# Scoring a quarter of the keys on VectorE instead of TensorE in a one-token attention decode

## Chip, cores, metric

One core of a Trainium2 chip. The metric is the device time of one execution, in microseconds; where several runs are given, the median. In the profile PE is TensorE (PEld its weight loads), DVE is VectorE, ACT is ScalarE, POOL is GpSimd, SP is SyncE, which here issues the loads. The granted clock is the share of its full speed at which the profile says that TensorE was allowed to run. A packet is one piece of a transfer; those of K and V have 16 KB each.

## The reference

```python
q = (x @ wq).reshape(1, 1, 32, 128).transpose(0, 2, 1, 3)      # x: 1 x 512
scores = einsum("bhqd,bhkd->bhqk", q, k_cache) * 128 ** -0.5   # k_cache: 1 x 32 x 65536 x 128, bf16
p = softmax(scores)
a = einsum("bhqk,bhkd->bhqd", p, v_cache).reshape(1, 1, 4096) @ wo
b = (silu(x @ w_gate) * (x @ w_up)) @ w_down                   # 512 -> 1792 -> 512
out = g * a + (1 - g) * b                                      # g = sigmoid(sum(x * gate_w))
```

K and V are 537 MB each. Everything else is small. One token reads all of it once, so the floor is the time of the loads.

## The kernel before

Per head there are 512 key blocks of 128 keys, in eight chunks of 64 blocks; a chunk of K or V is one 2 MB load into a slot of a ring. K lies with the keys on the partitions, and this kernel transposes it for the scores: TensorE transposes eight blocks into a PSUM bank, VectorE or ScalarE (in turn) copies the bank to SBUF, and TensorE multiplies each transposed block by q. For the values, V is the stationary operand as it lies. A "step" of the PE program is one group of eight transposes, eight value matmuls of an earlier head and eight score matmuls of the group two steps back.

```python
NSLOT = 9; NPT = 5; NKT = 6; LAG_QK = 2; LAG_PV = 12
...
jobs = [wq, wq, k0, wg, wu, wd, k1, ..., k8, v0, k9, v1, ...]      # (shortened) V eight chunks behind K
for i, job in enumerate(jobs):                                     # SP
    if i >= NSLOT:
        w(*free_of(jobs[i - NSLOT]))      # k: all transposed;  v: all value matmuls of the chunk done
    sp.dma_start(view(job), source(job)).then_inc(ld[i % NSLOT], 16)
...
for g in range(1, NG, 2):                                          # ScalarE: odd groups
    h, r = divmod(g, GPH)
    if r == 9 and h >= 1:
        softmax(h - 1)                    # waits for nbias (GpSimd), then Exp over 512 columns
    w("tdone", g + 1)
    ...
    nc.scalar.activation(KT[:, g % NKT, :], kt_ps(g), ACT.Copy, bias=0.0).then_inc(sm["ev_a"], 1)   # L244
...
for g in range(0, NG, 2):                                          # VectorE: even groups
    if r == 4 and h >= 1:
        top(h - 1)                        # reduce_max of the head's scores, then GpSimd's all-reduce
    ...
    nc.vector.tensor_copy(KT[:, g % NKT, :], kt_ps(g)).then_inc(sm["ev_d"], 1)                      # L307
...
for g in range(n_steps):                                           # TensorE
    if g < NG: transposes(g)              # L352
    if 0 <= g - first_pv < NG: values(g - first_pv)                # L383, first_pv = GPH + LAG_PV
    if 0 <= g - LAG_QK < NG: scores(g - LAG_QK)                    # L366
    if g == mid: ...                      # out_proj of heads 0..30, after the first group of the last V chunk
```

Of the kernel before, what the change touches and what calls it, by code (L numbers as in the profile page):

```python
# [4 lines left out]

P = 128
GB = 8
NSLOT = 9
NPT = 5
NKT = 6  # L10
LAG_QK = 2
LAG_PV = 12

ALU = mybir.AluOpType
ACT = mybir.ActivationFunctionType
BF16 = mybir.dt.bfloat16
F32 = mybir.dt.float32
AX_X = mybir.AxisListType.X
# [4 lines left out]
def bass_gated_mix__mha_block_cached__swiglu_ffn__decode_kernel(  # L23
# [13 lines left out]
    _, H, S, Dh = A_k_cache.shape  # L37
# [3 lines left out]
    Dc = D // 128  # L41
    FC = F // 128
    NC_H = S // P
    assert NC_H <= 512
    CB = min(64, NC_H)
    NCH = NC_H // CB
    GPC = CB // GB
    GPH = NC_H // GB
    NG = H * GPH
    SCALE = float(Dh) ** -0.5  # L50
    SLOT = CB * 128

    with ExitStack() as ctx:
        def sb(name, shape, dt):
            return ctx.enter_context(nc.sbuf_tensor(name, shape, dt))
# [28 lines left out]
        oTn = sb("oTn", [P, max(H, 16)], BF16)  # L84
        fin = sb("finrow", [P, D], BF16)
        pcol = sb("pcol", [P, 2, NC_H], BF16)
        KT = sb("KT", [P, NKT, GB * 128], BF16)
        ring = sb("ring", [P, NSLOT, SLOT], BF16)

# [18 lines left out]
        for s in range(NK):  # L108
            jobs.append(("k", s))
            if s == 0:  # L110
                jobs += [("wg", 0), ("wu", 0), ("wd", 0)]
            if s >= NCH:
                jobs.append(("v", s - NCH))
        for s in range(NK - NCH, NK):
            if s == NK - NCH + min(2, NCH - 1):
                jobs += [("wo", i) for i in range(NOW)]
            jobs.append(("v", s))
# [16 lines left out]
        def source(job):  # L134
# [7 lines left out]
            if kind == "v":  # L142
# [3 lines left out]
        ld = [sem(f"ld{i}") for i in range(NSLOT)]  # L146
        names = ("s_x s_id0 s_ident s_ones s_xT s_xTb s_z s_e1 s_c s_q s_qTb s_h s_sig s_gu s_b s_brow "
                 "tdone ev_d ev_a qkdone pvdone s_mx s_ar s_nb expdone s_L s_li s_otn s_otl s_a s_a1 "
                 "s_fin s_out s_bs").split()
        sm = {n: sem(n) for n in names}  # L150

        def free_of(job):
            kind, i = job
            if kind == "wq":
                return "s_q", 1
            if kind in ("wg", "wu"):
                return "s_h", 1
            if kind == "wd":
                return "s_b", 1
            if kind == "k":  # L160
                return "tdone", (i + 1) * GPC
            if kind == "v":
                return "pvdone", i + 1
            raise AssertionError(kind)

        class Waits:
# [13 lines left out]

        def ev_of(g):

            return ("ev_d" if g % 2 == 0 else "ev_a"), g // 2 + 1

        def kt_ps(g):
            return psT[:, g % NPT, :].bitcast(BF16)
# [3 lines left out]
        @block.sync  # L190
        def _(sp):
            w = Waits(sp)
            sp.dma_start(xrow[0:1, :], A_x.rearrange("a b d -> (a b) d")).then_inc(sm["s_x"], 16)
            sp.dma_start(gwrow[0:1, :], gate_w.rearrange("(a d) -> a d", a=1)).then_inc(sm["s_x"], 16)
            for i, job in enumerate(jobs):
                if i >= NSLOT:
                    w(*free_of(jobs[i - NSLOT]))
                sp.dma_start(view(job), source(job)).then_inc(ld[i % NSLOT], 16)  # L198
            w("s_fin", 1)
            sp.dma_start(out.rearrange("a b d -> (a b) d"), fin[0:1, :]).then_inc(sm["s_out"], 16)  # L200
            w("s_out", 16)
# [17 lines left out]
        @block.scalar  # L219
        def _(act):  # L220
            w = Waits(act)
            w("s_z", 1)
            nc.scalar.activation(sc[0:1, 1:2], sc[0:1, 0:1], ACT.Exp, scale=-1.0).then_inc(sm["s_e1"], 1)

            def softmax(h):
                w("s_nb", h + 1)
                if h >= 2:
                    w("pvdone", (h - 1) * NCH)
                nc.scalar.activation(pcol[:, h % 2, :], psS[:, h % 2, 0:NC_H], ACT.Exp,  # L229
                                     bias=nbias[:, h:h + 1], scale=SCALE,  # L230
                                     accum_out=rsum[:, h:h + 1]).then_inc(sm["expdone"], 1)

            for g in range(1, NG, 2):
                if g == 2 * GPC + 1 or (2 * GPC + 1 >= NG and g == NG - 1):
                    w("s_h", 1)
                    nc.scalar.activation(hbuf[:, 0, 0:FC], psS[:, 1, 0:FC], ACT.Exp,
                                         scale=-1.0).then_inc(sm["s_sig"], 1)
                h, r = divmod(g, GPH)
                if r == 9 and h >= 1:
                    softmax(h - 1)  # L240
                w("tdone", g + 1)
                if g >= NKT:
                    w("qkdone", g - NKT + 1)
                nc.scalar.activation(KT[:, g % NKT, :], kt_ps(g), ACT.Copy, bias=0.0).then_inc(sm["ev_a"], 1)  # L244
            softmax(H - 1)

        @block.vector
        def _(dve):
# [14 lines left out]
                                           accum_out=sc[0:1, 0:1]).then_inc(sm["s_z"], 1)  # L263
            w("s_xT", 1)
            nc.vector.tensor_copy(xTb[:, 0:Dc], psS[:, 0, 0:Dc]).then_inc(sm["s_xTb"], 1)
            w("s_e1", 1)
            chain(nc.vector.tensor_scalar_add(sc[0:1, 2:3], sc[0:1, 1:2], 1.0))
            settle()
# [6 lines left out]
            def ffn():  # L275
# [7 lines left out]
                nc.vector.tensor_tensor(guT[:, 0:FC], hbuf[:, 0, 0:FC], psS[:, 1, 16:16 + FC],  # L283
                                        ALU.mult).then_inc(sm["s_gu"], 1)

            def top(h):
                w("qkdone", (h + 1) * GPH)
                nc.vector.reduce_max(mxs[:, h:h + 1], psS[:, h % 2, 0:NC_H], AX_X).then_inc(sm["s_mx"], 1)  # L288

            def ffn_out():  # L290
# [2 lines left out]
                nc.vector.tensor_scalar(brow[0:1, :], psO[0:1, 0:D], sc[0:1, 4:5], None,  # L293
                                        ALU.mult).then_inc(sm["s_brow"], 1)

            for g in range(0, NG, 2):
                if g == 2 * GPC + 2 or (2 * GPC + 2 >= NG and g == NG - 2):
                    ffn()
                if g == 3 * GPC or (3 * GPC >= NG and g == NG - 2):
                    ffn_out()  # L300
                h, r = divmod(g, GPH)
                if r == 4 and h >= 1:
                    top(h - 1)
                w("tdone", g + 1)
                if g >= NKT:
                    w("qkdone", g - NKT + 1)
                nc.vector.tensor_copy(KT[:, g % NKT, :], kt_ps(g)).then_inc(sm["ev_d"], 1)  # L307
            top(H - 1)

            w("s_L", 1)  # L310
# [13 lines left out]
        def _(pe):  # L324
# [11 lines left out]
            for h in range(H):  # L336
                for c in range(Dc):
                    last = mm(psS[:, 1, h:h + 1], view(("wq", c // CQ))[:, c % CQ, h * Dh:(h + 1) * Dh],  # L338
                              xTb[:, c:c + 1], start=(c == 0), stop=(c == Dc - 1))
            last.then_inc(sm["s_q"], 1)  # L340
            w("s_ident", 1)

            def transposes(g):
                c, r = divmod(g, GPC)
                w.job(("k", c))
                if g >= NPT:
                    w(*ev_of(g - NPT))
                src = view(("k", c))
                dst = kt_ps(g)
                for k in range(GB):  # L350
                    b = r * GB + k
                    last = nc.tensor.transpose(dst[:, k * 128:(k + 1) * 128], src[:, b * 128:(b + 1) * 128],  # L352
                                               ident[:])
                last.then_inc(sm["tdone"], 1)
# [13 lines left out]
                last.then_inc(sm["qkdone"], 1)  # L368

            def values(g):  # L370
                c, r = divmod(g, GPC)
                h, rh = divmod(g, GPH)
                if rh == 0:
                    w("expdone", h + 1)
                w.job(("v", c))
                if g == 0:
                    w("s_brow", 1)
                src = view(("v", c))
                acc = psO[:, h:h + 1] if h < H - 1 else psT[:, 1, 0:1]
                for k in range(GB):  # L380
                    b = r * GB + k
                    col = rh * GB + k
                    last = mm(acc, src[:, b * 128:(b + 1) * 128], pcol[:, h % 2, col:col + 1],  # L383
                              start=(col == 0), stop=(col == NC_H - 1))
                if r == GPC - 1:
                    last.then_inc(sm["pvdone"], 1)

            def ffn_in():
# [23 lines left out]
                   start=(h == 0), stop=(h == H - 1))  # L412

            first_pv = GPH + LAG_PV
            n_steps = max(NG + LAG_QK, NG + first_pv)
            mid = NG + first_pv - GPC
            for g in range(n_steps):
                if g == min(GPC + GPC // 2, NG - 1):
                    ffn_in()
                if g == min(2 * GPC + GPC // 2, NG - 1):  # L420
                    ffn_down()
                if g < NG:
                    transposes(g)
                if 0 <= g - first_pv < NG:
                    values(g - first_pv)
                if 0 <= g - LAG_QK < NG:
                    scores(g - LAG_QK)
                if g == mid:
                    w("s_otn", 1)
                    for h in range(H - 1):  # L430
                        out_proj(h)
            w("s_otl", 1)
            mm(psT[0:1, 0, 0:D], oTn[:, H - 1:H], view(("wo", (H - 1) // HO))[:, (H - 1) % HO, :],
               start=(H == 1), stop=True).then_inc(sm["s_a"], 1)
# [28 lines left out]
```

## Time and profile before

| | before |
|---|---|
| time, median of 3 runs | 2740.23 us (2731.75 to 2740.33) |
| busy share: PE, ACT, DVE | 94%, 39%, 27% |
| data moved | 1094 MB, 400 GB/s on average |
| 16 DMA engines, share of the span in the load queue's packets | 97.1% |
| granted TensorE clock, mean | 0.539 |

TensorE and the DMA engines both look full. These are lines of the page: the span, the busy times, the granted clock in tenths and the moved GB/s in 40 slices, the load queue (q1) and one queue that fetches instructions (q8), with packets, MB and share.

```profile
span 2736.7 us, 103879 instructions
...
PE 2569.2 (94%) x49442; PEld 2554.8 (93%) x49442; DVE 731.8 (27%) x1073; ACT 1068.3 (39%) x1091; POOL 21.8 (1%) x71
...
PEclk8755556555565555555556655555555555555555
...
GB/s 398 418 406 404 394 394 414 401 424 412 391 411 401 408 423 398 398 382 400 405 397 414 418 397 404 405 394 417 404 386 408 395 402 381 398 408 399 388 394 302
...
q1 hardware_dynamic: 81270, 1087.67, 97.1%
q8 instruction: 386, 6.32, 0.9%
...
PE 80%; issue 14%; DVE 2%; DMA 2%; ACT 1%; POOL 1%; SPq 1%; POOLq 0%; ACTq 0%
```

The last line is the chain that ended last, by engine: 80% of it is PE work and 2% is waiting for a load. Between the first slice and the last the GB/s vary from 381 to 424.

The waits of the engines (who waited for what: us in total, times, longest): PE lost 15 us to K loads, all of it at the start, and 96 us to ScalarE's copy, three microseconds once a head; ScalarE in turn had waited 181 us for nbias:

```profile
ACT pcol L229 <- POOL nbias L215: 181.0, 32, 11.3
...
PE psS L366 <- ACT KT L244: 96.5, 32, 4.9
...
PE psT L352 <- DMA ring<-in_A_k_cache_dram: 14.8, 2, 13.5
```

The load queue's own waits: SP stood nearly all the time at a slot that value matmuls had yet to free.

```profile
SPq L198 <- PE psO L383: 2376.7, 248, 17.4
SPq L198 <- PE psT L352: 55.5, 35, 6.1
```

One step of PE in the timeline (start, duration, line). Ends of matmuls are modelled and overlap; the starts give the pace: 3.37 to 4.65 is 1.28 us, so a chunk of eight steps takes 10.24 us.

```profile
1003.37 1.01 PE L352 MATMUL psT<-ident,ring 128*128 128x128 bf16 x8
1004.18 0.40 PE L383 MATMUL psO<-pcol,ring 128*128 128x1 bf16 x8
1004.44 0.35 PE L366 MATMUL psS<-qTb,KT 128*128 128x1 bf16 x8
1004.65 1.01 PE L352 MATMUL psT<-ident,ring 128*128 128x128 bf16 x8
```

The stretches view (length, busy us of PE, PEld, DVE, ACT and POOL, then granted clock, DMA share, GB/s). The first stretch is the only one with many loads queued, because few slots are in use yet:

```profile
36.00:115.00 79.00, 65.45 (x1412) 62.90 (x1413) 28.07 (x44) 39.33 (x41) 0.64 (x2) 0.82 1.01 425
115.00:1315.00 1200.00, 1144.95 (x22034) 1142.55 (x22032) 325.89 (x473) 477.76 (x488) 9.00 (x28) 0.53 0.99 403
1315.00:2500.00 1185.00, 1137.09 (x21658) 1134.90 (x21657) 320.36 (x465) 469.96 (x480) 9.00 (x28) 0.52 0.99 402
```

And the load issues (count, KB, median us from issue to landing). A 2 MB load takes 5 us at full rate, so a K load found about one load before it:

```profile
ring<-in_A_k_cache_dram SPq DMA_DIRECT2D x256, 2048.0 KB, 10.3
ring<-in_A_v_cache_dram SPq DMA_DIRECT2D x256, 2048.0 KB, 14.9
```

### The profile page before, as it was taken

To read this page: it belongs to the slowest core of one execution; us is meant where nothing else is said; L and a number is where in the kernel's file an instruction comes from. 1 tells how busy PE (TensorE), PEld (TensorE's weight loads), DVE (VectorE), ACT (ScalarE), POOL (GpSimd) and SP (SyncE) were. 2 spreads that over 40 slices of the span, in tenths; PEclk is the share of its full clock that TensorE was granted. 3 is DMA by queue.
4 is the path that set the end of the run, shared out by engine and by line. 5 is a ranking of instruction groups with operands and counts; after the bars stand their busy time and mean duration, and the time that the engine had idled before them with its cause. 6 is when DMAs were issued, how large, how long until landed. Compare 5 with 4: busy or idle time off the path is not lost.

```text
span 2736.7 us, 103879 instructions
## 1 busy us (share of the span) xinstructions
PE 2569.2 (94%) x49442; PEld 2554.8 (93%) x49442; DVE 731.8 (27%) x1073; ACT 1068.3 (39%) x1091; POOL 21.8 (1%) x71
## 2 busy tenths in 40 slices
PE   5899999999999999999999899999999999999997
PEld 5899999999989999999999899999999999999996
DVE  2322222222222222222222222222222222222221
ACT  2433334433343433333334433344333333334331
POOL 0000000000000000000000000000000000000000
PEclk8755556555565555555556655555555555555555
DMA  9999999999999999999999999999999999999997
GB/s 398 418 406 404 394 394 414 401 424 412 391 411 401 408 423 398 398 382 400 405 397 414 418 397 404 405 394 417 404 386 408 395 402 381 398 408 399 388 394 302
DMA packets 81695, 1094.32 MB, mean 400 GB/s; under 512 B 8307, under 2 KB 14198, under 8 KB 15222
## 3 DMA queue, kind: packets, MB, share of 16 engines
q1 hardware_dynamic: 81270, 1087.67, 97.1%
q8 instruction: 386, 6.32, 0.9%
q14 instruction: 39, 0.32, 0.0%
HBM read 1087.64 MB, written 0.00 MB: 397 GB/s over the span
## 4 chain that ended last, share of the span: by engine, by line
PE 80%; issue 14%; DVE 2%; DMA 2%; ACT 1%; POOL 1%; SPq 1%; POOLq 0%; ACTq 0%
PE psT L352 54%; PE psS L366 14%; PE psO L383 12%; ACT KT L244 1%; DMA ring<-in_A_k_cache_dram 1%; DVE KT L307 1%; DVE mxs L288 1%; DMA ring<-in_A_v_cache_dram 1%; SPq L198 1%; POOL amx L213 0%; PE psT L411 0%; POOL nbias L215 0%; ACT pcol L229 0%; PE psT L383 0%; PE psO L404 0%
## 5 line engine op out<-in xcount | busy, mean ns | idle before, releaser
L352 PE MATMUL psT<-ident,ring 128*128 128x128 bf16 x16384 | 1999.8, 300 | 20.2 <-DMA ring<-in_A_k_cache_dram 14.8
L244 ACT ACTIVATE KT<-psT 128x1024 bf16<-128x1024 bf16 x1024 | 1044.9, 1024 | 1451.9 <-PE psT L352 1451.9
L352 PEld LDWEIGHTS psT<-ident,ring 128*128 128x128 bf16 x16384 | 1518.8, 135 | 20.9 <-DMA ring<-in_A_k_cache_dram 13.6
L307 DVE COPY KT<-psT 128x1024 bf16<-128x1024 bf16 x1024 | 708.4, 692 | 1943.1 <-PE psT L352 1943.1
L366 PE MATMUL psS<-qTb,KT 128*128 128x1 bf16 x16384 | 720.6, 165 | 107.8 <-ACT KT L244 96.5
L383 PEld LDWEIGHTS psO<-pcol,ring 128*128 128x128 bf16 x15872 | 811.6, 115 | 7.3 <-issue 7.3
L383 PE MATMUL psO<-pcol,ring 128*128 128x1 bf16 x15872 | 782.0, 170 | 6.0 <-issue 6.0
L366 PEld LDWEIGHTS psS<-qTb,KT 128*128 128x128 bf16 x16384 | 594.9, 103 | 111.8 <-ACT KT L244 100.4
L229 ACT ACTIVATE pcol<-psS,nbias 128x512 bf16<-128x512 f32 x32 | 22.0, 687 | 181.0 <-POOL nbias L215 181.0
L213 POOL PARTITION_ALL_REDUCE amx<-mxs x32 | 12.2, 382 | 2329.8 <-DVE mxs L288 2329.8
L383 PEld LDWEIGHTS psT<-pcol,ring 128*128 128x128 bf16 x512 | 13.9, 103 | 17.5 <-ACT pcol L229 9.6
L383 PE MATMUL psT<-pcol,ring 128*128 128x1 bf16 x512 | 14.3, 165 | 16.8 <-ACT pcol L229 9.6
L288 DVE TENSOR_REDUCE mxs<-psS 128x1 f32<-128x512 f32 x32 | 21.8, 681 | 2.1 <-PE psS L366 2.1
L338 PE MATMUL psS<-xTb,ring 128*128 128x1 bf16 x128 | 3.6, 165 | 11.6 <-DMA ring<-in_A_wq_dram 11.6
L338 PEld LDWEIGHTS psS<-xTb,ring 128*128 128x128 bf16 x128 | 3.5, 104 | 11.6 <-issue 11.6
L215 POOL TENSOR_SCALAR nbias<-amx 128x1 f32<-128x1 f32 x32 | 8.4, 261 | 342.1 <-issue 342.1
L411 PE MATMUL psT<-ring,oTn 128*1 128x512 bf16 x31 | 9.2, 471 | 0.0
L411 PEld LDWEIGHTS psT<-ring,oTn 128*1 128x1 bf16 x31 | 3.0, 99 | 5.8 <-issue 3.5
L229 ACT ACTIVATION_READ_ACCUMULATOR pcol<-psS,nbias 128x1 f32 x32 | 6.2, 193 | 0.0
L311 DVE RECIPROCAL Li<-Lt 128x32 f32<-128x32 f32 x1 | 0.4, 353 | 20.5 <-POOL Lt L217 20.5
L317 DVE TENSOR_TENSOR oTn<-psT,Li 128x1 bf16<-128x1 f32 x1 | 0.2, 161 | 20.6 <-PE psT L383 20.6
L273 DVE CAST qTb<-psS 128x32 bf16<-128x32 f32 x1 | 0.2, 192 | 14.0 <-PE psS L338 14.0
(32 smaller groups left out, 18.4 us busy)
## 6 DMA issues: line engine op xcount, KB each, us to landing
ring<-in_A_k_cache_dram SPq DMA_DIRECT2D x256, 2048.0 KB, 10.3
ring<-in_A_v_cache_dram SPq DMA_DIRECT2D x256, 2048.0 KB, 14.9
ring<-in_A_wq_dram SPq DMA_DIRECT2D x2, 2048.0 KB, 10.1
ring<-in_A_wo_dram SPq DMA_DIRECT2D x2, 2048.0 KB, 14.4
ring<-in_B_w_gate_dram SPq DMA_DIRECT2D x1, 1792.0 KB, 22.2
ring<-in_B_w_up_dram SPq DMA_DIRECT2D x1, 1792.0 KB, 26.2
ring<-in_B_w_down_dram SPq DMA_DIRECT2D x1, 1792.0 KB, 30.6
xrow<-in_A_x_dram SPq DMA_DIRECT2D x1, 1.0 KB
```

What stands on the lines that cost most here:

```text
L198: sp.dma_start(view(job), source(job)).then_inc(ld[i % NSLOT], 16)
L213: nc.gpsimd.partition_all_reduce(amx[:, h:h + 1], mxs[:, h:h + 1], P, RMAX).then_inc(sm["s_ar"], 1)
L215: nc.gpsimd.tensor_scalar_mul(nbias[:, h:h + 1], amx[:, h:h + 1], -SCALE).then_inc(sm["s_nb"], 1)
L229: nc.scalar.activation(pcol[:, h % 2, :], psS[:, h % 2, 0:NC_H], ACT.Exp, bias=nbias[:, h:h + 1], scale=SCALE, accum_out=rsum[:, h:h + 1]) ...
L244: nc.scalar.activation(KT[:, g % NKT, :], kt_ps(g), ACT.Copy, bias=0.0).then_inc(sm["ev_a"], 1)
L288: nc.vector.reduce_max(mxs[:, h:h + 1], psS[:, h % 2, 0:NC_H], AX_X).then_inc(sm["s_mx"], 1)
L307: nc.vector.tensor_copy(KT[:, g % NKT, :], kt_ps(g)).then_inc(sm["ev_d"], 1)
L338: last = mm(psS[:, 1, h:h + 1], view(("wq", c // CQ))[:, c % CQ, h * Dh:(h + 1) * Dh], xTb[:, c:c + 1], start=(c == 0), stop=(c == Dc - 1))
L352: last = nc.tensor.transpose(dst[:, k * 128:(k + 1) * 128], src[:, b * 128:(b + 1) * 128], ident[:])
L366: last = mm(psS[:, h % 2, col:col + 1], KT[:, g % NKT, k * 128:(k + 1) * 128], qTb[:, h:h + 1], start=True, stop=True)
L383: last = mm(acc, src[:, b * 128:(b + 1) * 128], pcol[:, h % 2, col:col + 1], start=(col == 0), stop=(col == NC_H - 1))
L411: mm(psT[0:1, 0, 0:D], oTn[:, h:h + 1], view(("wo", h // HO))[:, h % HO, :], start=(h == 0), stop=(h == H - 1))
```

## The change

The intent: 16 of every 64 key blocks no longer go through TensorE for their scores. VectorE multiplies them by q, broadcast to all partitions (the keys are on the partitions, so no transpose is needed), and sums each row. q is broadcast once at the start by 32 matmuls. ScalarE alone now copies transposes. A tenth slot, V loaded two chunks later behind K, and the softmax one group later in ScalarE's program (a head has 48 groups now, not 64) go with it.

```diff
-NSLOT = 9
+NSLOT = 10
-LAG_PV = 12
+LAG_PV = 15
+V_LAG = 2
+ND = 16
@@
+    CBT = CB - ND
+    GPC = CBT // GB                      # 6 groups a chunk instead of 8
@@ load order
-            if s >= NCH:
-                jobs.append(("v", s - NCH))
+            if s >= NCH + V_LAG:
+                jobs.append(("v", s - NCH - V_LAG))
@@ a K slot is free
-                return "tdone", (i + 1) * GPC
+                return ("tdone", (i + 1) * GPC), ("s_tt", i + 1)
@@ ScalarE
-            for g in range(1, NG, 2):
+            for g in range(NG):
-                if r == 9 and h >= 1:
+                if r == min(10, GPH - 1) and h >= 1:
                     softmax(h - 1)
@@ VectorE, once a chunk, in place of the copies
+                kb = view(("k", c))[:, CBT * 128:CB * 128].rearrange("p (a b) -> p a b", b=128)
+                qb = qbc[:, h, :].unsqueeze(1).broadcast_to([P, ND, 128])
+                nc.vector.tensor_tensor(prod[:], kb, qb, ALU.mult).then_inc(sm["s_tt"], 1)
+                w("s_tt", c + 1)
+                nc.vector.reduce_sum(sD[:, h % 2, j * ND:(j + 1) * ND], prod[:], AX_X).then_inc(sm["s_rd"], 1)
@@ before the head's maximum
+                nc.vector.tensor_copy(psS[:, h % 2, NCT:NC_H], sD[:, h % 2, :]).then_inc(sm["s_cp"], 1)
@@ TensorE, once
+                for c in range(Dc):
+                    last = mm(psT[:, i % NPT, 0:TQ], xb[:, c, :],
+                              view(("wq", c // CQ))[:, c % CQ, i * TQ:(i + 1) * TQ], ...)
... (value matmuls re-ordered to match the columns; allocations, semaphores and waits cut)
```

## The prediction

> **What bounds it now.** Two near-equal limits: TensorE and the load queue.
>
> TensorE: the page gives PE 94% busy. In mid-run the timeline shows a step of 1.28 us: 8 transposes (0.85), 8 value matmuls (0.21), 8 score matmuls (0.21), at a granted clock near half. A 64-block chunk is 8 steps, 10.24 us; 256 chunks make 2621 us. The waits view adds 96 us, 32 times 3 us, on the ScalarE copy (L244): once a head ScalarE waits for nbias (181 us in all) and transposes run out of PSUM.
>
> DMA: busy 97%, 400 GB/s, 1094 MB. PE almost never waits for a load, yet this isn't DMA at its ceiling. The queue's own waits show SP waiting 2377 us for value matmuls to free a slot: it issues a K and a V load together every 10.2 us, when some 5 us of the load before is left. In the packet records a typical 16 KB packet takes 611 ns; packets over 700 ns come mostly 1 to 3 us after such an issue (up to 20% there, 1% later); the mean is 640. The windows view shows what a full queue does: 36 to 115 us, with four or five loads waiting, ran at 425 GB/s, the rest at 400 to 406. The Trainium skill, "DMA: Bandwidth & Descriptors" (section Bandwidth), measured 425 GB/s for a 16 MB load; this trace agrees.
>
> **What the change does.** A chunk has 48 blocks to transpose and score instead of 64. PE per chunk, estimated from the step: 48 x 134 ns + 64 x 27 ns = 8.1 us, 2080 in all: 20% slack. ScalarE copies six groups a chunk, 6 x 1.02 us plus softmax, under 7 us. VectorE loses 708 us of copies and gains a 2048-element product into F32 and a 2048-element row sum. The Trainium skill, "VectorE: DVE Perf Modes" (perf-mode tier table), has both at one element per cycle, 2.29 us for 2048; here reduce_max over 512 takes 0.68 us. Estimate: 4.5 us a chunk, 1150 us in all. The q broadcast adds 32 N=512 matmuls, 7 to 14 us before the first transpose, hidden because ten loads (50 us) are queued. The softmax comes later after the scores' end, so its wait nearly goes.
>
> No engine needs over 8.1 us a chunk, and 5 K + 5 V slots leave five or more loads waiting. The kernel becomes DMA-bound with a queue that never runs low.
>
> **Sum.** The first six loads land by 35 us, as now. Then 511 K/V loads at 4.98 us (slowest DMA engine in the full-queue stretch; 4.91 for the fastest) = 2545; two wo loads 12; tail after the last V 14. Total 2606.
>
> Predicted **2608 us**, 80% range **2585 to 2655**. Faster by over 2%: 0.94; within 2%: 0.05; slower: 0.01.
>
> **What would show it.** DMA share 97 to 100%, 415 to 425 GB/s in every slice, times to landing 25 us or more; PE busy 75 to 80%, its main waits now on k_cache and v_cache loads; ACT L244 near 1570 us busy; product and row sum near 2.2 us each, DVE 40 to 45%; PE's 96 us of waits on ScalarE gone.
>
> **What would make it wrong.** A full queue doesn't sustain 425 GB/s (at 410: about 2695); the F32 product's SBUF traffic slows packets; slow packets come from the issues themselves, not a short queue; the single evicting engine or a late softmax stalls PE beyond the slots' slack.

## The result, and the profile after

The ratios below are computed as the mean time of one kernel's fast runs over that of the other's fast runs of the same rounds, so they are not quite the ratio of the medians quoted.

| | before | after |
|---|---|---|
| median | 2740.28 us (4 runs) | 2622.38 us (4 runs) |
| lowest to highest | 2731.75 to 2743.25 | 2621.72 to 2622.64 |
| ratio | | 0.9574 (95%: 0.9553 to 0.9596) |

The runs of after agree within a microsecond; those of before spread over 11.5. That is a clue by itself, taken up below.

The page after:

```profile
span 2620.5 us, 87632 instructions
...
PE 2120.4 (81%) x41281; PEld 2051.0 (78%) x41282; DVE 1208.0 (46%) x598; ACT 1585.7 (61%) x1607; POOL 25.3 (1%) x71
...
PEclk8755565555555555555555555555555555555555
...
GB/s 397 425 424 425 425 426 425 425 425 425 426 424 426 424 426 425 425 426 425 425 422 422 421 421 419 421 420 424 419 419 420 418 424 419 421 420 418 421 370 276
...
q1 hardware_dynamic: 81270, 1087.67, 98.6%
q8 instruction: 322, 5.28, 0.8%
...
DMA 82%; PE 15%; issue 1%; SPq 1%; ACT 1%; POOL 0%; DVE 0%; POOLq 0%; ACTq 0%
```

The chain that ended last has changed from 80% PE to 82% DMA, and the rate is now flat: 425 GB/s for the first half, about 420 for the second. The engines' waits show the same exchange. PE waits for K loads, and the wait for ScalarE's copy has shrunk from 96 to 6 us:

```profile
PE psT L411 <- DMA ring<-in_A_k_cache_dram: 411.6, 240, 8.3
...
ACT pcol L251 <- POOL nbias L237: 30.2, 14, 9.2
...
PE psO L442 <- DMA ring<-in_A_v_cache_dram: 25.4, 39, 3.0
...
PE psS L425 <- ACT KT L270: 5.8, 3, 4.8
```

SP still waits for slots most of the time, 2283.5 us now (the first two lines). But loads queued before a wait keep the engines at work: a load now lands over 40 us after its issue, so seven or eight are queued ahead of it.

```profile
SPq L220 <- PE psO L442: 1428.9, 243, 7.2
SPq L220 <- PE psT L411: 854.6, 252, 11.2
...
ring<-in_A_k_cache_dram SPq DMA_DIRECT2D x256, 2048.0 KB, 42.5
ring<-in_A_v_cache_dram SPq DMA_DIRECT2D x256, 2048.0 KB, 41.2
```

(The first two lines are the queue's waits, the last two the page's load issues.) PE's steps in the timeline: 1.28 us, then one with 16 value matmuls, then the wait for the next K chunk. A step with 16 value matmuls takes 1.50 us where no wait follows it (1000.07 to 1001.57, not shown). Three groups take 1.28 + 1.28 + 1.50 = 4.06 us, a chunk of six 8.1, as the prediction's estimate had it.

```profile
1002.85 1.01 PE L411 MATMUL psT<-ident,ring 128*128 128x128 bf16 x8
1003.65 0.40 PE L442 MATMUL psO<-pcol,ring 128*128 128x1 bf16 x8
1003.91 0.35 PE L425 MATMUL psS<-qTb,KT 128*128 128x1 bf16 x8
1004.13 1.01 PE L411 MATMUL psT<-ident,ring 128*128 128x128 bf16 x8
1004.93 0.61 PE L442 MATMUL psO<-pcol,ring 128*128 128x1 bf16 x16
1005.41 0.35 PE L425 MATMUL psS<-qTb,KT 128*128 128x1 bf16 x8
1007.59 1.03 PE L411 MATMUL psT<-ident,ring 128*128 128x128 bf16 x8 [1.83 <-DMA ring<-in_A_k_cache_dram]
```

The same stretches as before:

```profile
36.00:115.00 79.00, 66.84 (x1259) 57.42 (x1260) 57.67 (x32) 62.19 (x68) 4.23 (x2) 0.80 1.01 425
115.00:1315.00 1200.00, 992.07 (x19341) 968.74 (x19339) 562.22 (x270) 748.76 (x755) 9.63 (x30) 0.52 1.01 425
1315.00:2500.00 1185.00, 973.56 (x18917) 950.98 (x18916) 553.56 (x266) 733.04 (x740) 9.61 (x30) 0.52 1.00 420
```

And the groups of the moved work (busy us, mean ns of one, then idle time before). The product takes 2.29 us and the row sum 2.29, ScalarE's copies 1.03 each:

```profile
L270 ACT ACTIVATE KT<-psT 128x1024 bf16<-128x1024 bf16 x1536 | 1562.0, 1030 | 922.3 <-PE psT L411 921.7
...
L329 DVE TENSOR_TENSOR prod<-ring,qbc 128x2048 f32<-128x2048 bf16 x256 | 586.7, 2292 | 1299.9 <-DMA ring<-in_A_k_cache_dram 1298.8
...
L331 DVE TENSOR_REDUCE sD<-prod 128x16 f32<-128x2048 f32 x256 | 585.2, 2286 | 8.7
```

**One thing that the prediction had not seen.** A load raises its semaphore sixteen times, and the trace has the time of each. There are 16 DMA engines, and we read each of these landings as one engine's; the trace doesn't say which engine it was. In the kernel before, the sixteen landings of one load mostly lie within 1 to 4 us (median 2.6). In the kernel after they drift apart. For the 200th load they are, in us after the first:

```
0.0  0.0  0.1  0.5  1.5  1.5  3.5  8.1 | 23.2 23.3 23.4 23.4 24.7 24.8 24.9 25.2
```

Eight engines lag by 25 us, and the lag had grown steadily: between the 29th and the 200th load the first landing moves on by 4.895 us a load, the last by 5.014. From about load 270 the spread stays at 32 to 34 us: the faster engines have then nearly finished all eight queued loads and wait for the next issue, which comes at the pace of the slow eight. The trace bears this out: the first landing comes 31 us after the issue (median of the loads issued from 115 to 600 us), but 8.3 us after it from 1315 us on. That is the 420 GB/s of the second half; the last landing goes on at 5.014 us a load (loads 200 to 500). The rate in GB/s is an average of sixteen engines, the time is that of the slow eight. The experiments look for their cause too.

### The profile page after: what moved, and what is told of

Its sections match the earlier page's. It is cut to its first block, busy times and chain, and to the rows that moved or that the text cites. A ratio compares the mean times of both kernels' runs of the same rounds, so it can differ in the third digit from the quotient of the medians.

```text
span 2620.5 us, 87632 instructions
## 1 busy us (share of the span) xinstructions
PE 2120.4 (81%) x41281; PEld 2051.0 (78%) x41282; DVE 1208.0 (46%) x598; ACT 1585.7 (61%) x1607; POOL 25.3 (1%) x71
## 3 DMA queue, kind: packets, MB, share of 16 engines
q1 hardware_dynamic: 81270, 1087.67, 98.6%
## 4 chain that ended last, share of the span: by engine, by line
DMA 82%; PE 15%; issue 1%; SPq 1%; ACT 1%; POOL 0%; DVE 0%; POOLq 0%; ACTq 0%
DMA ring<-in_A_k_cache_dram 65%; DMA ring<-in_A_v_cache_dram 17%; PE psT L411 10%; PE psO L442 2%; PE psS L425 2%; SPq L220 1%; ACT KT L270 1%; PE psT L470 0%; PE psT L442 0%; PE psO L463 0%; PE psS L454 0%; POOL amx L235 0%; POOL nbias L237 0%; DVE finrow L366 0%; DVE mxs L338 0%
## 5 line engine op out<-in xcount | busy, mean ns | idle before, releaser
L270 ACT ACTIVATE KT<-psT 128x1024 bf16<-128x1024 bf16 x1536 | 1562.0, 1030 | 922.3 <-PE psT L411 921.7
L411 PE MATMUL psT<-ident,ring 128*128 128x128 bf16 x12288 | 1523.5, 303 | 412.1 <-DMA ring<-in_A_k_cache_dram 411.6
L411 PEld LDWEIGHTS psT<-ident,ring 128*128 128x128 bf16 x12288 | 1153.1, 137 | 432.8 <-DMA ring<-in_A_k_cache_dram 431.5
L329 DVE TENSOR_TENSOR prod<-ring,qbc 128x2048 f32<-128x2048 bf16 x256 | 586.7, 2292 | 1299.9 <-DMA ring<-in_A_k_cache_dram 1298.8
L442 PEld LDWEIGHTS psO<-pcol,ring 128*128 128x128 bf16 x15872 | 692.6, 111 | 54.0 <-DMA ring<-in_A_v_cache_dram 38.0
L442 PE MATMUL psO<-pcol,ring 128*128 128x1 bf16 x15872 | 690.2, 169 | 26.9 <-DMA ring<-in_A_v_cache_dram 25.4
L331 DVE TENSOR_REDUCE sD<-prod 128x16 f32<-128x2048 f32 x256 | 585.2, 2286 | 8.7
L425 PE MATMUL psS<-qTb,KT 128*128 128x1 bf16 x12288 | 540.9, 165 | 10.1 <-ACT KT L270 5.8
L425 PEld LDWEIGHTS psS<-qTb,KT 128*128 128x128 bf16 x12288 | 445.8, 104 | 18.2 <-ACT KT L270 17.7
L442 PE MATMUL psT<-pcol,ring 128*128 128x1 bf16 x512 | 14.8, 165 | 34.2 <-DMA ring<-in_A_v_cache_dram 34.2
L442 PEld LDWEIGHTS psT<-pcol,ring 128*128 128x128 bf16 x512 | 14.2, 103 | 35.2 <-DMA ring<-in_A_v_cache_dram 31.6
L336 DVE COPY psS<-sD 128x128 f32<-128x128 f32 x32 | 9.1, 284 | 7.9 <-PE psS L425 7.9
L384 PEld LDWEIGHTS psS<-xTb,ring 128*128 128x128 bf16 x128 | 3.5, 104 | 11.5 <-issue 11.5
```

Of the source, the lines that this page charges most:

```text
L329: nc.vector.tensor_tensor(prod[:], kb, qb, ALU.mult).then_inc(sm["s_tt"], 1)
L331: nc.vector.reduce_sum(sD[:, h % 2, j * ND:(j + 1) * ND], prod[:], AX_X).then_inc(sm["s_rd"], 1)
L411: last = nc.tensor.transpose(dst[:, k * 128:(k + 1) * 128], src[:, b * 128:(b + 1) * 128], ident[:])
L425: last = mm(psS[:, h % 2, col:col + 1], KT[:, g % NKT, k * 128:(k + 1) * 128], qTb[:, h:h + 1], start=True, stop=True)
L442: last = mm(acc, src[:, b * 128:(b + 1) * 128], pcol[:, h % 2, col:col + 1], start=(j == 0 and b == 0), stop=(j == NCH - 1 and b == CB - 1))
```

## The experiments

Three questions: what bounded the kernel before; which part of the change did the work; and what makes eight DMA engines slow, which now sets the time. The kernel after was not run again in these jobs, which used chips 0, 2, 5 and 10, so comparisons with it, and of variants from different jobs, take for granted that chips matter little once loads set the time. This is argued and not tested by one kernel on two chips. What supports it: a_nd24 on chip 0 and a_tail24 on chip 2, whose loads and instruction packets are the same in number, have their last landing at 2603.7 and 2603.4 us. All results were correct. A few of the runs of before were slow and are left out of the ratios. Within each variant of the kernel after, the four runs lie within 2 us.

### b_slots10: the tenth slot alone

```diff
 # kernel before
-NSLOT = 9
+NSLOT = 10
```

> The kernel before with a tenth slot and nothing else. Theory (TensorE is what bounds the kernel before; the short load queue only makes packets slow): within 1% of before, 2715 to 2745 us, PE still about 94% busy with its 96 us of waits on the ScalarE copy, mean 16 KB packet falls from 640 towards 620 ns and the DMA engines show idle time in its place. Rival (the short load queue is the limit, and the gain of the change came from the extra slot): 2620 to 2660 us.

Measured: 2730.14 us (2713.43 to 2751.53); before in the same rounds 2726.40 (2712.89 to 2747.86); ratio 0.9994 (0.9914 to 1.0074). PE waited 92.6 us for the ScalarE copy. The time half of the theory holds. The packet half missed: 16 KB packets stayed slow (a mean of 638 ns in this trace and in that of before). K and V still found only one or two loads queued (times to landing 14.8 and 10.1 us).

Four of the seven runs of before in these rounds, with their granted clocks: 2712.89 us at 0.554, 2722.41 at 0.550, 2726.40 at 0.547, 2745.46 at 0.536. On the whole, the higher the clock granted to TensorE, the shorter the time; the other three runs are out of this order by less than 4 us. In kernels that loads bound, the clock doesn't show: a_nd8 below ran at 0.544 to 0.566, and its four times lie within 1.2 us.

### b_latesoft: no work moved, only the stall taken out

```diff
 # kernel before
-NSLOT = 9
+NSLOT = 10
-LAG_PV = 12
+LAG_PV = 20
-            if s >= NCH:
-                jobs.append(("v", s - NCH))
+            if s >= NCH + 1:
+                jobs.append(("v", s - NCH - 1))
-                if r == 9 and h >= 1:
+                if r == 15 and h >= 1:
                     softmax(h - 1)
```

> The kernel before with ten slots, the softmax taken at ScalarE's 15th group of the next head instead of the 9th, the value matmuls 8 groups later and V loaded one slot later to match. No work leaves TensorE. Theory: the once-a-head stall on nbias goes (PE waits on the ScalarE copy under 15 us instead of 96), so 2635 to 2665 us, about three quarters of the gain without any VectorE scoring, and still PE-bound. Rival (the stall is off the critical path, or the DMA rate and not the stall set the time): within 1% of 2740 us.

Measured: 2664.35 us (2659.87 to 2666.65), ratio to before 0.9771 (0.9719 to 0.9823). The stall is gone. This is the ScalarE wait that is left, with the chain that ended last; PE has no wait on ScalarE's copy in the list at all (PEld 0.2 us):

```profile
ACT pcol L229 <- POOL nbias L215: 11.8, 2, 11.3
...
PE 97%; DMA 2%; SPq 1%; issue 0%; ACT 0%; DVE 0%
```

So the once-a-head stall was on the critical path: 62 us between the medians, over half of the change's gain, with no arithmetic moved. The interval of the ratio excludes 1 but not 0.98, so that it is faster is shown, and that it is so by 2% is not. Of the other parts of this edit, the slot alone gave nothing, and PE's wait for K loads was as short before as now (14.8 and 14.2 us), so the changed order of the loads had nothing to save there. At an equal clock it might have been more; this rests on one pair of profiles. The profiled run of b_slots10 ran at 0.525 and that of b_latesoft at 0.520, with spans of 2749.7 and 2664.9: 84.8 us apart, close to the 92.6 us of stall. The other runs of before and of b_slots10 had 0.535 to 0.554, all of b_latesoft 0.519 to 0.524. PE is then busy 2608 of 2665 us (98%), and PE work is 97% of the chain, where it was 80% before: this kernel is bound by TensorE's work.

### a_short: the offload without the extra slot and the V lag

```diff
 # kernel after
-NSLOT = 10
+NSLOT = 9
-V_LAG = 2
+V_LAG = 0
```

> The kernel after with 9 slots and V loaded where it was before (no lag): the offload to VectorE alone, with a load queue of about two loads at each issue. Theory (taking work off TensorE is what matters; the queue only has to be never empty on the slowest DMA engine): 2620 to 2650 us. Rival (the deep queue is needed for the rate): 2670 to 2720 us, with packets over 650 ns at 5% or more and 400 to 408 GB/s.

Measured: 2622.26 us (2621.93 to 2622.67), ratio to before 0.9618 (0.9568 to 0.9669). The same as the kernel after, to 0.1 us. Times to landing are short:

```profile
ring<-in_A_k_cache_dram SPq DMA_DIRECT2D x256, 2048.0 KB, 15.7
ring<-in_A_v_cache_dram SPq DMA_DIRECT2D x256, 2048.0 KB, 20.3
```

So two to three loads were queued at an issue instead of eight, and the spread between the engines stops at 8 us instead of 33. The rate is about 420 GB/s from the sixth of the 40 slices on, where the kernel after has it only in its second half, and the time is the same: the last landings, those of the slow eight, follow each other at 5.016 us a load here and at 5.014 in the kernel after (loads 200 to 500). The new slot and the V lag did nothing for the time. What is left in a_short is the 16 blocks, the later softmax and the later value matmuls (LAG_PV) together; no run takes the blocks from TensorE and leaves the stall.

### a_nd8 and a_nd24: less and more on VectorE

```diff
 # kernel after                      # a_nd8          # a_nd24
-ND = 16                             +ND = 8          +ND = 24
-LAG_PV = 15                         +LAG_PV = 18     +LAG_PV = 13
```

> The kernel after with only 8 of 64 blocks on VectorE (LAG_PV 18). PE needs an estimated 56 x 134 + 64 x 27 ns = 9.2 us a chunk, less than the 10.03 us that a K and a V load take. Theory (DMA-bound as soon as PE is below the loads): 2628 us, +-3, 6 above the kernel after for the 32 instruction packets more, with PE about 92% busy and still waiting on loads. Rival (PE and the loads have to be well apart): 2640 to 2680 us.

> The kernel after with 24 of 64 blocks on VectorE (LAG_PV 13). PE gets yet less work, VectorE about 6.9 us a chunk. Theory (DMA-bound, pace set by the eight slowest DMA engines, which lag the others by 0.116 us a load): 2612 to 2624 us; if that lag is the fetch of instructions (322 packets of 16 KB over eight engines), 32 packets fewer save about 6 us, so 2616. Rival 1 (PE still matters): 2560 to 2600 us. Rival 2 (the F32 products' traffic slows loads): over 2630 us.

Measured: a_nd8 2629.08 us (2628.23 to 2629.38), ratio to before 0.9631; a_nd24 2616.10 us (2615.48 to 2617.32), ratio 0.9596. With 8, 16 and 24 blocks: 2629.1, 2622.3, 2616.1. PE busy goes 89% (92% was expected), 81%, 71% of the span; VectorE 25%, 46%, 67%. If TensorE's work still set the time, 8 blocks more a chunk would have bought 8 x 0.134 us x 256 = 274 us (an estimate from the step); they bought 6.5. The rival of a_nd8 and both rivals of a_nd24 fall. What changes by the same small amount is the number of instruction packets: 354, 322, 290.

### a_dummy: more PE instructions, same result

```diff
 # kernel after; zc is a column of zeros
+                    if k % 2 == 0:
+                        mm(acc, src[:, b * 128:(b + 1) * 128], zc[:, 0:1], start=False, stop=False)
```

> The kernel after with 32 more matmuls a chunk that add zero to the value sums: 8192 weight loads and 8192 matmuls, about 0.9 us of PE a chunk, which PE has free (8.1 of 10.0 us). Same result. Theory (eight DMA engines also fetch the instructions and so fall behind; the slope between 16 and 24 blocks was about 0.18 us for a 16 KB packet): 64 packets more, so 11 to 12 us more, 2634 us, and the lag of the eight engines per load grows from 0.116 to about 0.139 us. Rival (those eight engines are slow of themselves, and instructions are not the cause): 2622 +- 2 us.

Measured: 2632.65 us (2631.66 to 2633.60), ratio to before 0.9645 (0.958 to 0.9711). 64 instruction packets more (386), 10.3 us more than the kernel after, with PE still waiting 212 us for K. The lag (table below) is 0.146 us a load where 0.139 was expected. The rival, slow engines that have nothing to do with instructions, falls. Whether PE's instructions or its reading did it is left to later runs.

### a_poolwaits: more instructions on another engine

```diff
 # kernel after, GpSimd, once a head after nbias
+                for _ in range(512):
+                    pool.wait_ge(sm["s_ident"], 1)
```

> The kernel after with 16384 more instructions on GpSimd's sequencer (512 waits a head on a semaphore that has long been reached), which touch no data. Theory (fetching instructions costs load time whoever fetches): also 64 packets more; if they come through the same eight engines, about 2634 us, if through others that have time to spare, 2622 and a smaller lag between the engines. Rival (what slowed a_dummy was PE's reading, or an engine that is slow of itself): 2622 +- 2 us with the lag between the engines unchanged.

Measured: 2622.17 us (2621.68 to 2623.22), unchanged. Two waits made one instruction, so it was half the instructions expected; and they came over another queue:

```profile
q8 instruction: 322, 5.28, 0.8%
q14 instruction: 104, 0.85, 0.1%
```

q14 had 40 packets in the kernel after, so 64 were added, of 8 KB each. The sixteen landings of the 200th load now read

```
0.0  0.0  0.2  0.9  1.4  4.5  8.6 19.2 | 23.1 23.3 23.3 23.5 24.8 24.8 25.0 25.0
```

One landing that was among the early eight now lags by 19.2 us; the slow eight are where they were. (The landings don't name their engines, so which one moved is not known.) By the letter this fits neither side: the theory's second alternative asked for a smaller lag, and the lag from first to last is unchanged, as the rival had it; but the rival had no engine moving. We read it as that second alternative: these instructions were fetched through one engine that had time to spare. It doesn't by itself exclude that PE's reading slowed a_dummy. a_pewaits64 does.

### a_tail24: 24 blocks, and out_proj earlier

```diff
 # a_nd24
-                if done_v == NV - VPC:
+                if done_v == NV - min(6, NCH) * VPC:
                     w("s_otn", 1)
                     for h in range(H - 1):
                         out_proj(h)
```

> 24 blocks on VectorE, and out_proj of the first 31 heads moved from before the last V chunk to before the last six, where PE waits 15 us for the loads. Theory (after the last V lands only its own value matmuls and the last head's projection remain, 5.5 us instead of 11): 2610 us, +-2, 6 less than with 24 blocks alone. Rival (the tail is hidden elsewhere): 2616 us.

Measured: 2610.37 us (2610.16 to 2610.72), ratio to before 0.9564 (0.9499 to 0.9629). In the kernel after 11.1 us pass between the last landing (2609.4) and the end (2620.5); here it is 5.1 (2603.4 to 2608.5). **This is the version that beats both kernels, before and after**: 12.0 us under the kernel after, of which 6.0 are the earlier last landing and 6.0 the shorter tail. (Its ratio to before, 0.9564, can't be set beside the 0.9574 of after: the runs of before in different rounds differ by more than that, as do their clocks.)

### a_pewaits64 and a_pewaits128: PE instructions that do nothing

The kernels so far changed TensorE's instructions and its reading together. This pair changes the instructions alone.

```diff
 # a_tail24, after each group of eight value matmuls
+                for _ in range(8):               # 16 in a_pewaits128
+                    pe.wait_ge(sm["s_ident"], 1)
```

> a_tail24 with 64 waits a chunk more on TensorE's sequencer, for a semaphore that has long been reached: they read no data and compute nothing. In a_poolwaits two such waits made one instruction, so 8192 instructions, 32 packets of TensorE's queue. Theory (the eight DMA engines fall behind because they fetch TensorE's instructions): 2615.5 to 2617 us, 6 above a_tail24's 2610.4, with the lag per load between the engines up by a tenth (290 to 322 packets). Rival (they fall behind because of what TensorE reads or does): 2610 to 2611 us and the lag unchanged.

> The same with 128 waits a chunk, 64 packets. Theory: 2621 to 2623 us, if the waits themselves don't fill TensorE's free time of some 2.9 us a chunk (then longer, with PE no longer waiting for loads). Rival: 2610 to 2611 us.

Measured: a_pewaits64 2618.08 us (2618.02 to 2618.67), ratio to before 0.9651 (0.9573 to 0.9728), 7.7 above a_tail24 (5.9 in the last landing, 1.9 in a longer tail); a_pewaits128 2647.40 us (2647.28 to 2648.31), ratio 0.9759 (0.9658 to 0.9861), 37 above. The first is 1 us above its range, and its lag (table below) rose by 17% where a tenth was expected. The second is a miss of the total for another reason, named in the expectation as possible but in a different place: the loads ended on time, but where only value matmuls are left, PE's sequencer needs about 0.9 us for eight matmuls and their waits, 7.2 us a V chunk against 4.9 for its load, so the program ended 30.8 us after the last landing. The last landing is the clean measure, and it moved as the theory says: 2603.4, 2609.3 and 2614.7 us for 290, 322 and 354 packets of TensorE's queue.

All variants of the kernel after that have ten slots, side by side. "Lag" is how far the slowest engine's landings fall behind the fastest's per load, between the 20th and the 200th load:

| kernel | q8 packets | lag, us a load | last V landing, us |
|---|---|---|---|
| a_tail24 | 290 | 0.104 | 2603.4 |
| a_nd24 | 290 | 0.103 | 2603.7 |
| after | 322 | 0.122 | 2609.4 |
| a_poolwaits | 322 | 0.121 | 2609.8 |
| a_pewaits64 | 322 | 0.122 | 2609.3 |
| a_nd8 | 354 | 0.138 | 2615.9 |
| a_pewaits128 | 354 | 0.133 | 2614.7 |
| a_dummy | 386 | 0.146 | 2619.4 |

Lag over packets is 0.00036 to 0.00039 us in all eight, so between 290 and 386 packets the lag is nearly proportional to the packets. Whether the added instruction multiplies data, multiplies zeros or waits for nothing makes little difference: 2609.4 and 2609.3 us with 322 packets, 2615.9 and 2614.7 with 354. From a_tail24 to a_dummy a packet costs (2619.4 - 2603.4) / 96 = 0.167 us of the kernel's time.

### a_tail32: half of the blocks

```diff
 # kernel after, with out_proj moved as in a_tail24
-ND = 16
+ND = 32
-LAG_PV = 15
+LAG_PV = 10
-NSLOT = 10
+NSLOT = 9
-V_LAG = 2
+V_LAG = 0
```

> Half of the blocks (32 of 64) on VectorE, out_proj moved as in a_tail24, and nine slots with V loaded without lag[...]. LAG_PV 10. VectorE then needs an estimated 2 x 4.43 us a chunk plus 1.1 us a head, 9.0 of 10.0 us. Theory (32 instruction packets fewer through the eight engines, VectorE just below the loads): 2604 to 2606 us. Rival (VectorE's late row sums hold K slots and the softmax back, with so shallow a queue): 2615 to 2660 us.

Measured: 2622.93 us (2622.41 to 2624.07), ratio to before 0.9635 (0.9569 to 0.9702): 12.6 us worse than a_tail24. The timeline shows that the loss is made once. VectorE needs 8.9 us a chunk, while in the first head only K is loaded, a chunk every 5 us; VectorE finishes scoring the first head at 113 us, the softmax of head 0 follows, and until then V chunks can't be used and all slots are taken. SP issued no load between 109.0 and 133.8 us, and the DMA engines stood idle for 18 us. From 215 us on the rate is 422 to 424 GB/s, as elsewhere. The theory's steady state held and its start did not; the rival has the cause (late sums holding back slots and the softmax), but only for the first head. Without the 18 us the time would be within the theory's range (an estimate: 2622.9 - 18 = 2604.9).

## Why the prediction was right

Predicted 2608 us with 2585 to 2655; measured 2622.38.

- **"The kernel becomes DMA-bound with a queue that never runs low."** Shown: the chain that ended last is 82% DMA, PE waits 412 us for K loads, the queue's share is 98.6%, times to landing are over 40 us, the rate is 418 to 426 GB/s in all slices but the first and the last two, and 8 blocks more or fewer on TensorE move the time by 6.5 us, not by 270.
- **Costs of the moved work.** PE 8.1 us a chunk estimated and read back; product and row sum 2.29 us each (predicted near 2.2; the Trainium skill's 2.29 us for 2048 elements, "VectorE: DVE Perf Modes", perf-mode tier table, agrees with the trace); ScalarE's copies 1562 us (1570 predicted). PE busy came out at 81% (75 to 80 predicted) and VectorE at 46% (40 to 45).
- **"Its wait nearly goes"** (the softmax): 181 to 30 us, and PE's wait on ScalarE 96 to 6.
- **The sum.** The sixth load landed at 34.4 us (35 predicted) and the two wo loads took 11.8 (12). Two terms were mis-sized. The 511 K and V loads took 5.016 us each ((2609.4 - 34.4 - 11.8) / 511) and not 4.98: 18 us more. The tail was 11.1 us, not 14. The 4.98 was read from the stretch from 36 to 115 us, some 16 loads, probably too few to give the slowest engine's pace to 1%; and the prediction didn't ask why one engine was slower than another. The experiments put it down to the fetch of TensorE's own instructions. The two errors have opposite signs, so that 3 us of the 18 were hidden by luck.
- **What the prediction gave too much credit.** It let "5 K + 5 V slots" make the queue full. a_short has nine slots and no V lag and takes the same time. Relief for TensorE did the work: 16 blocks less, and the stall nearly gone. Nor were the two limits of its first line near equal in effect: with the stall taken out and all blocks still on TensorE (b_latesoft), PE was 97% of the chain and loads 2%.
- **What it read rightly but weighed too lightly.** It counted the stall on nbias as part of the old kernel's time. b_latesoft shows that taking out the stall alone gives 62 us of the 104 that a_short gives against the same runs of before (2726.40 to 2664.35 and to 2622.26).
- **Slow packets.** The prediction took them for the sign of a short queue, worth 6% of rate. Packets over 650 ns did fall, to 1% in the first half of the kernel after. But in its second half, and in a_short, 2 to 3% are slow and the time is unaffected. They may be packets of the faster engines, which have time; the packet records don't name the engine, so this is not shown. What makes a packet slow wasn't tested by itself.

Open: which eight engines fetch for TensorE, and why a 16 KB packet of instructions costs more than its size. 0.167 us of time on eight engines is 1.3 us of engine time (an estimate: 8 x 0.167), where a 16 KB packet of data takes 0.61. The packet records of the kernel after show the larger part of this: its 322 packets of q8 took 1.07 us each on average. Why they take longer than data, and what the rest is, no run here separates.

## What to carry to other kernels

When two resources are both near 95% busy, ask the chain and the waits, not the averages; then look for a stall that recurs (here once a head, behind a reduction on GpSimd), because moving a wait away may give over half of the gain (here 62 of 104 us). Once loads set the time, judge them by the pace of the slowest DMA engine's landings, not by GB/s, and count instructions: a fully unrolled program such as this one fetches its instructions through the same engines. And check the start and the tail by themselves: moving one projection into a gap gave about as much as another eighth of the scoring taken from TensorE, and an engine that keeps up on average may still be too slow for the first head.

## What the Trainium skill lacked or had wrong

- "Runtime: NRT & Kernel Launch", section "Instruction fetch mechanics", says that instruction memory is refilled in 16 KiB blocks and that crossing a block is "mostly hidden". The size agrees (82,563 PE and PEld instructions / 256 = 322.5; the trace has 322 packets). The cost was not hidden in a load-bound kernel: 0.167 us of its time for a block of TensorE's, an estimated 54 us (322 x 0.167, which carries the slope from 290 to 386 packets down to none), 2% of the whole. No page gives this cost beside loads, or says on how many engines it falls: the lag here is in eight of sixteen landings for TensorE's blocks, and in one for GpSimd's.
- "DMA: Bandwidth & Descriptors", section "Latency and other measured facts", has engines 7 and 15 as usually slower, with a guess that concerns loads issued from GpSimd. Here, with loads issued from SP, eight of sixteen landings fell behind, by 0.122 us in 5 us, and the cause was instruction fetch.
- No page gives the rate by how many loads are queued: 425 GB/s with four and more in the first stretch of the kernel before, 402 to 403 later with one or two (where TensorE set the time), 420 in a_short with two to three. But the kernel after, with seven or eight queued, also ran at 420 in its second half, so the number queued is not all that sets it.
